# Three part-filled expert blocks of the first batch dealt early, and block work re-rated over the batches, in a top-k attention and dropless MoE kernel

## Chip, cores and metric

One core of one Trainium2 chip. The metric is device time in microseconds (us), the median of several runs. A profiled execution is one further run, with its own time.

## The reference

Top-32 attention over 8 batches of 8 heads (sequence 576, head dimension 64), then a mixture of 8 experts over the 4608 resulting rows of 512, each row going to one expert, none dropped:

```python
scores = scale * np.matmul(q, k.transpose(0, 1, 3, 2))
kth = np.partition(scores, -top_k, axis=-1)[..., -top_k:-top_k + 1]
scores = np.where(scores >= kth, scores, -1000000000.0)
attn = softmax(scores); x = (attn @ v) as rows (4608, 512)
expert_idx = np.argmax(x @ w_gate, axis=1)      # w_gate 512 x 8
for e in range(E):                              # rows sorted by expert
    h = np.maximum(x_sorted[lo:hi] @ w1[e], 0.0)   # 512 -> 1024
    y_sorted[lo:hi] = h @ w2[e]                    # 1024 -> 512
return gate_w[:, None] * y                      # softmax weight of the chosen expert
```

All tensors are float32.

## The kernel before

**The scan.** Attention is done in 144 groups, 18 for each batch. A group holds two query tiles. For each, TensorE makes the scores (`sc`, L292), ScalarE copies them (`s`, L299), VectorE (DVE) folds them and finds the 32nd largest score by repeated max and replace (L306 to L362), ScalarE and GpSimd (POOL) turn what lies under the threshold into a large negative exponent (`low` L371, `w` L387, L396), ScalarE takes the exponential (L404), and TensorE transposes the weights (`wTm` L415, `wTl` L429) and multiplies by the values (`po` L450). Products run three groups ahead (`AHEAD`). `low` runs once in each group.

**End of a batch.** `ending` turns the outputs into rows, computes the gate logits, ranks rows by expert (`choice`, `ranks`, `places`), and scatters each batch's rows with five indirect transfers into `x_rows`, a DRAM buffer in which every expert has its own region of `CAP` rows. `run` holds how far each region is filled. These small DVE steps wait in the list `aside`; `search` calls `tick` between its own instructions, which issues one of them.

**Blocks.** 128 rows of one expert are a block. `block` transposes its rows (`xtp`, `xTs`), multiplies by `w1` (`ph`, L893, 32 matmuls) and by `w2` (`py`, L910, 8 matmuls), and stores the result to the rows' places in the output (L808). A block is yielded in `PIECES` = 16 pieces: eight of four `ph` matmuls and eight of one `py` matmul. Blocks of the batches so far are dealt while the scan of the next batches goes on: after batch b, `table` works out which full blocks exist and writes `new_of[b]` of them into slots, and SP reads expert and place from a slot and loads rows (L749), `w1` (L741) and `w2` (L743), each 2 MB, into two buffers each. The numbers of new blocks are fixed when the program is built, from `upto_of`: 0, 4, 4, 5, 4, 5, 4. A slot without a full block would point at an empty block.

**The rate.** In the loop over the groups a credit grows by `rate` for each tile, and as many pieces as it holds (by `share` of the tile's place) are put between that group's transposes and products. From group 13 (`FIRST`) of a batch on, the rate is that of the blocks dealt after the batch before:

```python
if at == FIRST and b:
    rate = new_of[b - 1] * PIECES / (U * NT)
```

In the last batch the credit is spread so that three blocks (`KEEP`) remain, which run while the last rows are routed. The instruction order of TensorE, ScalarE and DVE in the loop is that of the program text; SP's and POOL's is set by the scheduler of the framework.

**The end.** After the last batch ten blocks remain beside the three kept: `SURE` = 2 whole ones that `table` finds first, four long blocks (`HALVES`: a whole block and a half of 64 rows together, `long_block`) and `PLAIN` = 4 whole ones, dealt by `end_table`. `fill_up` writes zero rows behind each expert's last row, so that part-filled blocks can be multiplied. Only if blocks are left over, or the search is in doubt, is a branch taken that does the rest (`rare`).

Of the kernel before, what the change touches and what calls it, by code (L numbers as in the profile page):

```python
# [9 lines left out]
F32 = mybir.dt.float32  # L10
I32 = mybir.dt.int32
AF = mybir.ActivationFunctionType
ALU = mybir.AluOpType
# [24 lines left out]
def _inner(ap: bass.AP, n: int) -> bass.AP:  # L38
    return _ins(ap, len(ap.ap), n)
# [3 lines left out]
def kernel(  # L43
# [47 lines left out]
    nc = tc.nc  # L91
    B, U, P, _ = qk.shape
    N, Dm = out.shape
    S = N // B
    E = moe_w_gate.shape[1]
# [4 lines left out]
    ST = S - SM  # L100
# [5 lines left out]
    NT = 2 * NC + 1  # L106
    DT = Dm // P
    FT = F // P
    XW = Dm + 2
    EB = N // P  # L110
    NSLOT = EB + E - 1
    CAP = N + P
    EMPTY = E * CAP // P
# [1 line left out]
    assert N % P == 0 and TOP_K == 32 and DT == U and P == 2 * D  # L115
    scale = float(D) ** -0.5
    sure = [max(0, -((E * (P - 1) - S * (b + 1)) // P)) for b in range(B - 1)]
    upto_of = [max(0, (S * (b + 1) - E * ST) // P - 1) for b in range(B - 1)]
    upto_of = [max(a, c) if b else 0 for b, (a, c) in enumerate(zip(sure, upto_of))]
    new_of = [b - a for a, b in zip([0] + upto_of, upto_of)]  # L120
    assert all(n >= b - a for n, a, b in zip(new_of, [0] + sure, sure))
    LAST = NSLOT - sure[-1]
    HALVES = E // 2
    SURE = 2
    PLAIN = EB - upto_of[-1] - HALVES - SURE
    LONG = P + ST
    assert PLAIN >= 0 and (N - E * (P - 1) + P - 1) // P - upto_of[-1] >= SURE
    assert LAST - SURE + HALVES <= NSLOT and PLAIN + HALVES <= NSLOT

    k = SimpleNamespace()  # L130
# [86 lines left out]
    run = const.tile([P, E], F32, name="run")  # L217
    nc.vector.tensor_copy(run, e_at)
    rest_i = const.tile([1, 1], I32, name="rest_i")
    rare = const.tile([1, 1], F32, name="rare")  # L220
    slot_last = const.tile([1, 2, NSLOT], I32, name="slot_last")
    slot_long = slot_last[:, 0, NSLOT - 3 * E:].rearrange("o (i e) -> o i e", i=3)
    assert LAST - SURE <= NSLOT - 3 * E
    done = const.tile([1, E], F32, name="done")
    nc.vector.tensor_scalar_mul(done, e_at[0:1, :], 1.0 / P)
    slot_max = const.tile([1, 2], F32, name="slot_max")
    nc.vector.memset(slot_max[:, 0:1], float(E - 1))
    nc.vector.memset(slot_max[:, 1:2], float(EMPTY))
    upto_all = const.tile([1, E + 1], F32, name="upto_all")
# [97 lines left out]
    def through(steps):  # L327
        for _ in steps:
            pass
        if steps in aside:  # L330
            aside.remove(steps)
# [265 lines left out]
    def table(slot_i, n, last, riding=None):  # L597

        sm = k.small
        full = sm.tile([1, E], F32, name="full")  # L600
        ci = sm.tile([1, E], I32, name="ci")
        left = sm.tile([1, E], F32, name="left")
        past = sm.tile([1, NSLOT, E], F32, name="past", bufs=1)
        slot_f = sm.tile([1, 2, NSLOT], F32, name="slot_f", bufs=1)
        upto, step = upto_all, step_all

        def steps():
            if last:
# [12 lines left out]
            nc.vector.tensor_tensor(left, full, done, op=ALU.subtract)  # L621
            yield
            nc.vector.tensor_tensor_scan(upto[:, 1:], ones[0:1, 0:E], left, 0.0, op0=ALU.mult, op1=ALU.add)
            yield
            nc.vector.tensor_tensor(step[:, 0:E - 1], done[:, 1:E], full[:, 0:E - 1], op=ALU.subtract)
            yield
            nc.vector.tensor_tensor(
                past[:, 0:n, :], _inner(slots[:, 0:n], E), _ins(upto[:, 1:], 1, n), op=ALU.is_ge
            )
            yield  # L630
            nc.vector.tensor_reduce(slot_f[:, 0, 0:n], past[:, 0:n, :], axis=AX.X, op=ALU.add)
            yield
            nc.vector.tensor_tensor(past[:, 0:n, :], past[:, 0:n, :], _ins(step[:, :], 1, n), op=ALU.mult)
            yield
            nc.vector.tensor_reduce(slot_f[:, 1, 0:n], past[:, 0:n, :], axis=AX.X, op=ALU.add)
            yield
            nc.vector.scalar_tensor_tensor(
                out=slot_f[:, 1, 0:n], in0=slot_f[:, 1, 0:n], scalar=done[:, 0:1], in1=slots[:, 0:n],
                op0=ALU.add, op1=ALU.add,
            )  # L640
            yield
            nc.vector.tensor_tensor(slot_i[:, :, 0:n], slot_f[:, :, 0:n], _inner(slot_max[:, :], n), op=ALU.min)
            yield
            if last:
                nc.vector.tensor_copy(rest_i, upto[:, E:])
            else:
                nc.vector.tensor_scalar_min(upto, upto, float(n))
                yield
                nc.vector.tensor_tensor(left, upto[:, 1:], upto[:, 0:E], op=ALU.subtract)
                yield  # L650
                nc.vector.tensor_tensor(done, done, left, op=ALU.add)
                yield

        return steps()

    def counted():

# [11 lines left out]
    def end_table(slot_i, slot_l, n, half, full):  # L669
# [16 lines left out]
            v.tensor_scalar(to, to, what[:, 0:1], None, ALU.add)  # L686

        def steps():
            v.tensor_tensor_scan(hupto[:, 1:], ones[0:1, 0:E], half, 0.0, op0=ALU.mult, op1=ALU.add)
            v.tensor_tensor(left, full, done, op=ALU.subtract)  # L690
            v.tensor_scalar(take, hupto[:, 1:], float(HALVES), None, ALU.is_le)
            v.tensor_tensor(take, take, half, op=ALU.mult)
            v.tensor_tensor(take, take, left, op=ALU.min)
# [16 lines left out]
                out=slot_f[:, 1, 0:m], in0=slot_f[:, 1, 0:m], scalar=done[:, 0:1], in1=at[:, 0:m],  # L710
                op0=ALU.add, op1=ALU.add,
            )
            v.tensor_tensor(slot_i[:, :, 0:n], slot_f[:, :, 0:n], _inner(slot_max[:, :], n), op=ALU.min)
            yield
            v.tensor_tensor(past[:, 0:E, :], _inner(slots[:, 0:E], E), _ins(hupto[:, 1:], 1, E), op=ALU.is_ge)
            v.tensor_reduce(long_f[:, 0, :], past[:, 0:E, :], axis=AX.X, op=ALU.add)
# [220 lines left out]
    with fast:  # L937
        units = [(b, u) for b in range(B) for u in range(U)]
        unit.append(load_unit(*units[1]))
        for n in unit:  # L940
            load_values(n)
        nc.sync.dma_start(x_rows[EMPTY * P:(EMPTY + 1) * P, :], blank)

        work = [(b, g) for b in range(B) for u in range(0, U, 2) for g in groups(u)]
        per_batch = len(work) // B
# [1 line left out]
        waiting, loaded, coming, spare, scatters, stores = [], [], [], [], [], []  # L947
        current = None
        left = clock = 0

        def landed(n):
            return clock is None or clock - n.at >= ON_CHIP
# [59 lines left out]
        def ending(b, u):  # L1012
# [48 lines left out]
            yield "pool"  # L1061
            through(steps)
            scatters.extend(scattering(r, x))
            if b == B - 1:
                scatter(KC)
                slot_i = k.small.tile([1, 2, NSLOT], I32, name="slot_i")
                half, full = counted()
                through(table(slot_i, SURE, False, half))
                firsts = [(slot_i[0:1, 0, j:j + 1], slot_i[0:1, 1, j:j + 1]) for j in range(SURE)]
                ready = load_rows(SimpleNamespace(), firsts[0][1], True)  # L1070
# [15 lines left out]
            if b == B - 1:  # L1086
                spare.extend(coming[PLAIN:])
                del coming[PLAIN:]
                longs = [[slot_long[0:1, i, j:j + 1] for i in range(3)] for j in range(E)]
                spare.extend((expert, half) for expert, half, _ in longs[HALVES:])  # L1090
                coming[0:0] = [(expert, [full, half]) for expert, half, full in longs[:HALVES]]
                assert len(loaded) == 2 and not waiting
                fill_up()
                coming[0:0] = [(firsts[0][0], ready)] + [(expert, (piece,)) for expert, piece in firsts[1:]]
                scatter(0)
# [27 lines left out]
        def loop():  # L1123
# [9 lines left out]
            for i, (b, g) in enumerate(work):  # L1133
# [20 lines left out]
                at_place("rows")  # L1154
                at = i % per_batch
                if at == FIRST and b:
                    rate = new_of[b - 1] * PIECES / (U * NT)
                credit += rate * len(g)
                room = left
                if b == B - 1 and at >= ARRIVED:  # L1160
# [61 lines left out]
    with ExitStack() as outer:  # L1222
# [10 lines left out]
        with ExitStack() as st:  # L1233
# [44 lines left out]
                    put()  # L1278
                nc.vector.tensor_scalar_add(ids, ids, S)
            fill_up()  # L1280
            slot_i = slot_last
            for _ in table(slot_i, NSLOT, True):
                pass
            nc.sync.dma_start(slot_d.rearrange("(a n) o -> o a n", a=2), slot_i)
# [53 lines left out]
```

## Time and profile before

| | |
|---|---|
| median of 3 runs | 1337.66 us (1337.55 to 1337.73) |
| profiled execution, its own time | 1339.03 us |
| its span, first to last instruction | 1337.4 us |
| mean granted TensorE clock | 0.955 |
| TensorE busy | 1189.3 us (89%) |
| DVE busy | 1076.6 us (81%) |
| ScalarE busy | 930.8 us (70%) |
| POOL busy | 661.9 us (49%) |
| DMA | 214.36 MB, mean 160 GB/s |

Times of single instructions and stretches come from the profiled execution. Busy time of an engine is the union of its recorded instructions; an instruction that waits within its record counts as busy. The granted clock is the share of full speed that TensorE's throttle let through.

### The profile page before, as it was taken

To read this page: it belongs to the slowest core of one execution; us is meant where nothing else is said; L and a number is where in the kernel's file an instruction comes from. 1 tells how busy PE (TensorE), PEld (TensorE's weight loads), DVE (VectorE), ACT (ScalarE), POOL (GpSimd) and SP (SyncE) were. 2 spreads that over 40 slices of the span, in tenths; PEclk is the share of its full clock that TensorE was granted. 3 is DMA by queue.
4 is the path that set the end of the run, shared out by engine and by line. 5 is a ranking of instruction groups with operands and counts; after the bars stand their busy time and mean duration, and the time that the engine had idled before them with its cause. 6 is when DMAs were issued, how large, how long until landed. Compare 5 with 4: busy or idle time off the path is not lost. (4 is left out here: it accounts for less than half of the span.)

```text
span 1337.4 us, 24295 instructions
## 1 busy us (share of the span) xinstructions
PE 1189.3 (89%) x7570; PEld 831.4 (62%) x7570; DVE 1076.6 (81%) x4629; ACT 930.8 (70%) x2125; POOL 661.9 (49%) x805
## 2 busy tenths in 40 slices
PE   5667766766799999999999999999999999999995
PEld 3344443444466766676677666666677667699973
DVE  7999999999999999999999999999999932000000
ACT  4788788887888888888787888887778851111110
POOL 3454547555755665567555756475547642000000
PEclk9788788888899999999999999999999999999998
DMA  2000001001384348435855294329452739946790
GB/s 84 30 29 30 30 29 65 29 29 38 122 305 168 108 164 288 160 110 175 297 208 179 74 350 170 118 76 372 171 204 87 283 116 332 369 146 219 290 342 18
DMA packets 95563, 214.36 MB, mean 160 GB/s; under 512 B 4926, under 2 KB 25662, under 8 KB 95424
## 3 DMA queue, kind: packets, MB, share of 16 engines
q1 hardware_dynamic: 88800, 192.45, 40.8%
q0 software_dynamic: 6336, 19.97, 4.2%
q8 instruction: 61, 1.00, 0.3%
q14 instruction: 78, 0.64, 0.2%
q10 hardware_dynamic: 288, 0.30, 0.1%
HBM read 191.42 MB, written 21.80 MB: 159 GB/s over the span
## 5 line engine op out<-in xcount | busy, mean ns | idle before, releaser
L396 POOL TENSOR_TENSOR w<-s,w 128x576 f32<-128x576 f32 x288 | 410.2, 1444 | 418.4 <-ACT w L387 418.4
L893 PE MATMUL ph<-xTs,w 128*128 128x128 f32 x2048 | 250.2, 276 | 5.9 <-ACT xTs L790 5.9
L893 PEld LDWEIGHTS ph<-xTs,w 128*128 128x128 f32 x2048 | 239.1, 192 | 21.9 <-issue 14.6
L910 PE MATMUL py<-w,hT 128*128 128x512 f32 x512 | 236.2, 597 | 0.0
L404 ACT ACTIVATE w<-w,nbias 128x576 f32<-128x576 f32 x288 | 224.1, 792 | 3.0 <-POOL w L396 2.0
L292 PE MATMUL sc<-qkb 64*128 64x288 f32 (+1 forms) x1280 | 206.0, 473 | 9.5 <-ACT s L299 5.1
L387 ACT ACTIVATE w<-s,low 128x576 f32<-128x576 f32 x288 | 207.6, 768 | 4.7
L415 PE MATMUL wTm<-turn,w 128*128 128x128 f32 x1152 | 170.1, 287 | 32.0 <-ACT xl L468 21.4
L415 PEld LDWEIGHTS wTm<-turn,w 128*128 128x128 f32 x1152 | 132.0, 145 | 92.5 <-issue 34.4
L299 ACT COPY s<-sc 128x576 f32<-128x576 f32 x288 | 168.9, 640 | 10.4 <-PE sc L292 10.4
L1217 DVE CAST any_i<-pd 1x1 int32<-1x1 f32 x1 | 0.1, 145 | 207.9 <-PE pd L1215 207.9
L422 ACT COPY wT<-wTm 128x512 f32<-128x512 f32 x256 | 139.2, 604 | 39.3 <-PE wTm L415 39.2
L354 DVE MAX8 tops<-scr 128x8 f32<-128x168 f32 x576 | 162.8, 317 | 0.0
L450 PE MATMUL po<-wT,vb 128*64 128x288 f32 x1024 | 154.9, 450 | 0.4 <-ACT wTt L437 0.4
L354 DVE MAX8 tops<-few 128x8 f32<-128x144 f32 (+1 forms) x576 | 154.4, 300 | 0.0
L292 PEld LDWEIGHTS sc<-qkb 64*128 64x128 f32 (+1 forms) x1280 | 110.1, 195 | 65.4 <-issue 25.6
L910 PEld LDWEIGHTS py<-w,hT 128*128 128x128 f32 x512 | 90.7, 190 | 90.4 <-issue 89.2
L808 POOL DMA_INDIRECT out_dram<-y,xg x40 | 42.6, 1066 | 189.8 <-ACT y L869 82.5
L345 DVE MAX8 few<-l 128x8 f32<-128x288 f32 x288 | 127.3, 442 | 0.0
L450 PEld LDWEIGHTS po<-wT,vb 128*64 128x64 f32 x1024 | 74.2, 150 | 77.3 <-issue 26.0
L306 DVE TENSOR_TENSOR h<-s 128x576 f32<-128x576 f32 x144 | 114.8, 797 | 3.9 <-ACT s L299 3.7
L308 DVE TENSOR_TENSOR l<-s 128x576 f32<-128x576 f32 x144 | 108.0, 750 | 0.0
(175 smaller groups left out, 1649.8 us busy)
## 6 DMA issues: line engine op xcount, KB each, us to landing
w<-in_moe_w_dram SPq DMA_DIRECT2D x72, 2048.0 KB, 8.6
qkb<-in_qk_dram SPq DMA_DIRECT2D x31, 608.0 KB, 5.8
vb<-in_v_dram SPq DMA_DIRECT2D x32, 320.0 KB, 3.1
xg<-x_rows SPq DMA_DIRECT2D x36, 257.0 KB, 10.6
x_rows<-blank SPq DMA_DIRECT2D x5, 257.0 KB
x_rows<-blank POOLq DMA_DIRECT2D x4, 257.0 KB, 8.2
x_rows<-x,posi POOLq DMA_INDIRECT x40, 3.1
out_dram<-y,xg POOLq DMA_INDIRECT x40, 4.5
```

The lines of the kernel that those rows point to most:

```text
L292: nc.tensor.matmul(ps[rows, j, 0:HF], n.q[d, cols], n.k[d, keys], start=True, stop=True)
L299: lambda m=m, ps=ps: nc.scalar.copy(s[:, m, :, :], ps[:, :, 0:HF]) for m, ps in enumerate(got)
L345: nc.vector.max(out=f.few[:, m, QF + 8 * j:QF + 8 * j + 8], in_=away)
L354: nc.vector.max(out=tops[:, m, r * 8:(r + 1) * 8], in_=src[m])
L387: nc.scalar.activation(w[:, m, :], s[:, m, :, :].rearrange("p j k -> p (j k)"), AF.Relu, scale=-STEEP, bias=low[:, m:m + 1],)
L396: k.last_pool = in_turn(nc.gpsimd.tensor_tensor(w[:, m, :], s[:, m, :, :].rearrange("p j k -> p (j k)"), w[:, m, :], op=ALU.subtract)).ins
L404: nc.scalar.activation(w[:, m, :], w[:, m, :], AF.Exp, scale=scale, bias=nbias[:, m:m + 1], accum_out=n.z[:, c:c + 1])
L415: nc.tensor.transpose(pm[:, c * P:(c + 1) * P], w[:, m, first:first + P], ident)
L422: nc.scalar.copy(wT[:, :, m, q], pm4)
L450: nc.tensor.matmul(po[r, 0:HF], n.v[:, c, r], rhs, start=(c == 0), stop=(c == KC - 1))
L893: nc.tensor.matmul(ph[:, f, :], n.w1[:, 0, dt, fc * P:(fc + 1) * P], n.xT[:, dt, :], start=(dt == 0), stop=(dt == DT - 1),)
L910: nc.tensor.matmul(py, hT[:, f, :], n.w2[:, 0, f, :], start=(f == 0), stop=(f == FT - 1))
```

## The change

After the first batch, `filled_up` finds the three experts (`SOON`) with the most rows of that batch and sets their `run` to 128, so that each has a full block; the rows between were written with zeros at the start, where nine transfers of `blank` now stand in place of one. The blocks dealt become 3, 3, 4, 5, 4, 5, 3. The rate is worked out by `level`: the blocks at hand and still to come, over the batches that remain, at the lowest of the averages that the blocks at hand allow. `end_table` gets six steps that move half blocks without a whole partner to whole ones, and the tables of the end get room for more slots. `slot_max[:, :]` becomes `slot_max[:, 0:2]` in both tables (not shown).

```diff
+    SOON = 3
-    upto_of = [max(0, (S * (b + 1) - E * ST) // P - 1) for b in range(B - 1)]
-    upto_of = [max(a, c) if b else 0 for b, (a, c) in enumerate(zip(sure, upto_of))]
+    upto_of = [min((S * (b + 1) - E * ST) // P + 1, EB - E - 1) for b in range(B - 1)]
+    upto_of = [max(a, c) if b else SOON for b, (a, c) in enumerate(zip(sure, upto_of))]
-    LAST = NSLOT - sure[-1]
+    LAST = NSLOT + SOON - min(a + upto_of[-1] - b for a, b in zip(sure, upto_of))
-    PLAIN = EB - upto_of[-1] - HALVES - SURE
+    PLAIN = EB - upto_of[-1] - HALVES - SURE + 1
...
-    slot_last = const.tile([1, 2, NSLOT], I32, name="slot_last")
+    slot_last = const.tile([1, 2, NSLOT + SOON], I32, name="slot_last")
...
+    def filled_up():
+
+        most, few = k.small.tile([P, E], F32, name="left"), k.small.tile([P, E], F32, name="full")
+        nc.vector.tensor_tensor(few, run, e_at, op=ALU.subtract)
+        yield
+        nc.vector.max(out=most, in_=few)
+        yield
+        nc.vector.tensor_scalar(few, few, most[:, SOON - 1:SOON], float(P), ALU.is_ge, ALU.mult)
+        yield
+        nc.vector.tensor_tensor(few, few, e_at, op=ALU.add)
+        yield
+        nc.vector.tensor_tensor(run, run, few, op=ALU.max)
+        yield
...
         def steps():
+            v.tensor_tensor(left, full, done, op=ALU.subtract)
+            v.tensor_tensor(some, half, left, op=ALU.subtract)
+            v.tensor_scalar_max(some, some, 0.0)
+            v.tensor_tensor(half, half, some, op=ALU.subtract)
+            v.tensor_tensor(full, full, some, op=ALU.add)
+            v.tensor_tensor(left, left, some, op=ALU.add)
+            yield
             v.tensor_tensor_scan(hupto[:, 1:], ones[0:1, 0:E], half, 0.0, op0=ALU.mult, op1=ALU.add)
-            v.tensor_tensor(left, full, done, op=ALU.subtract)
...
-        nc.sync.dma_start(x_rows[EMPTY * P:(EMPTY + 1) * P, :], blank)
+        for r in [e * CAP for e in range(E)] + [EMPTY * P]:
+            nc.sync.dma_start(x_rows[r:r + P, :], blank)
...
+        def level(b):
+
+            have, sums = left / PIECES, []
+            for n, new in enumerate(new_of[b:] + [0], 1):
+                sums.append(have / n)
+                have += new
+            sums[-1] = (have - KEEP / PIECES) / (len(sums) - 1 + (per_batch - FIRST) / per_batch)
+            return min(sums)
...
             scatters.extend(scattering(r, x))
+            if b == 0:
+                steps = filled_up()
+                aside.append(steps)
+                yield "weights"
+                yield "pool"
+                through(steps)
             if b == B - 1:
...
                 if at == FIRST and b:
-                    rate = new_of[b - 1] * PIECES / (U * NT)
+                    rate = level(b) * PIECES / (U * NT)
...
-            slot_i = slot_last
+            slot_i = slot_last[:, :, 0:NSLOT]
```

More of the change, by code (lines that the diff above doesn't have):

```diff
@@ L117 @@
     sure = [max(0, -((E * (P - 1) - S * (b + 1)) // P)) for b in range(B - 1)]
-    upto_of = [max(0, (S * (b + 1) - E * ST) // P - 1) for b in range(B - 1)]
-    upto_of = [max(a, c) if b else 0 for b, (a, c) in enumerate(zip(sure, upto_of))]
+    upto_of = [min((S * (b + 1) - E * ST) // P + 1, EB - E - 1) for b in range(B - 1)]
+    upto_of = [max(a, c) if b else SOON for b, (a, c) in enumerate(zip(sure, upto_of))]
     new_of = [b - a for a, b in zip([0] + upto_of, upto_of)]
-    assert all(n >= b - a for n, a, b in zip(new_of, [0] + sure, sure))
-    LAST = NSLOT - sure[-1]
+    LAST = NSLOT + SOON - min(a + upto_of[-1] - b for a, b in zip(sure, upto_of))
     HALVES = E // 2
     SURE = 2
-    PLAIN = EB - upto_of[-1] - HALVES - SURE
+    PLAIN = EB - upto_of[-1] - HALVES - SURE + 1
     LONG = P + ST
-    assert PLAIN >= 0 and (N - E * (P - 1) + P - 1) // P - upto_of[-1] >= SURE
+    assert PLAIN >= 0 and E == 8 and SOON < E
     assert LAST - SURE + HALVES <= NSLOT and PLAIN + HALVES <= NSLOT
@@ L219 @@
     rest_i = const.tile([1, 1], I32, name="rest_i")
-    rare = const.tile([1, 1], F32, name="rare")
-    slot_last = const.tile([1, 2, NSLOT], I32, name="slot_last")
-    slot_long = slot_last[:, 0, NSLOT - 3 * E:].rearrange("o (i e) -> o i e", i=3)
-    assert LAST - SURE <= NSLOT - 3 * E
+    slot_last = const.tile([1, 2, NSLOT + SOON], I32, name="slot_last")
+    slot_long = slot_last[:, 0, NSLOT + SOON - 3 * E:].rearrange("o (i e) -> o i e", i=3)
+    assert LAST - SURE <= NSLOT + SOON - 3 * E
     done = const.tile([1, E], F32, name="done")
     nc.vector.tensor_scalar_mul(done, e_at[0:1, :], 1.0 / P)
-    slot_max = const.tile([1, 2], F32, name="slot_max")
+    slot_max = const.tile([1, 3], F32, name="slot_max")
+    rare = slot_max[:, 2:3]
     nc.vector.memset(slot_max[:, 0:1], float(E - 1))
@@ L641, in steps @@
             yield
-            nc.vector.tensor_tensor(slot_i[:, :, 0:n], slot_f[:, :, 0:n], _inner(slot_max[:, :], n), op=ALU.min)
+            nc.vector.tensor_tensor(slot_i[:, :, 0:n], slot_f[:, :, 0:n], _inner(slot_max[:, 0:2], n), op=ALU.min)
             yield
@@ L712, in steps @@
             )
-            v.tensor_tensor(slot_i[:, :, 0:n], slot_f[:, :, 0:n], _inner(slot_max[:, :], n), op=ALU.min)
+            v.tensor_tensor(slot_i[:, :, 0:n], slot_f[:, :, 0:n], _inner(slot_max[:, 0:2], n), op=ALU.min)
             yield
@@ L1091, in ending @@
                 coming[0:0] = [(expert, [full, half]) for expert, half, full in longs[:HALVES]]
-                assert len(loaded) == 2 and not waiting
+                assert len(loaded) == 2
                 fill_up()
```

## The prediction

> **What bounds the kernel now.** I read the 40 slices first. VectorE (DVE) is at 9 almost from the start, TensorE (PE) only from slice 11 on, and the granted TensorE clock is uneven before slice 11 and full after.
>
> ```profile
> PE   5667766766799999999999999999999999999995
> DVE  7999999999999999999999999999999932000000
> PEclk9788788888899999999999999999999999999998
> ```
>
> Then I cut the scan into stretches. One group is one search step over two query tiles; ScalarE's `low<-tops` (L371) runs once in each, so its 144 start times are the group boundaries, and block work is re-rated at group 13 of each batch (`FIRST`). The windows view between groups 13, 31, 49, 67, 85, 103, 121, 139 and 143, and from there to the end, gives (columns: stretch, its length, then busy time and count of PE, weight loads, DVE, ACT, POOL, then clock, DMA share, GB/s):
>
> ```profile
> 109.80:238.40 128.60, 90.64 (x538) 54.17 (x536) 128.00 (x557) 105.21 (x246) 74.58 (x93) 0.85 0.12 40
> 238.40:367.60 129.20, 92.15 (x554) 55.95 (x552) 129.20 (x572) 104.93 (x246) 74.40 (x93) 0.86 0.17 56
> 367.60:498.90 131.30, 127.01 (x862) 88.11 (x860) 131.30 (x573) 113.10 (x261) 78.45 (x96) 1.00 0.52 183
> 498.90:631.40 132.50, 129.22 (x878) 89.41 (x876) 132.16 (x572) 113.64 (x264) 80.94 (x97) 1.00 0.51 182
> 631.40:775.70 144.30, 142.59 (x958) 99.28 (x956) 140.94 (x579) 115.63 (x267) 87.63 (x98) 1.00 0.57 202
> 775.70:908.60 132.90, 129.62 (x880) 89.63 (x881) 131.77 (x566) 113.64 (x263) 82.52 (x97) 1.00 0.50 178
> 908.60:1052.90 144.30, 142.59 (x958) 99.30 (x956) 140.92 (x579) 115.65 (x267) 87.59 (x98) 1.00 0.55 197
> 1052.90:1079.00 26.10, 23.76 (x175) 18.11 (x176) 24.17 (x110) 23.91 (x58) 16.80 (x20) 1.00 0.89 333
> 1079.00:1337.40 258.40, 238.86 (x1423) 194.50 (x1422) 15.06 (x87) 47.58 (x87) 30.36 (x36) 0.97 0.64 229
> ```
>
> Eighteen groups without block work take 128.6 to 129.2 us, with 4 blocks 131.3 to 132.9, with 5 blocks 144.3. A block is 16 pieces (8 of four `ph` matmuls, 8 of one `py` matmul), so the first 64 pieces cost about 3 us in all and the next 16 cost 11.6. DVE busy is no proof here, since its recorded times contain waiting (L306 runs from 726 to 1853 ns), so I asked what ScalarE waits for. In 238.4 to 367.6 the longest is
>
> ```profile
> ACT low L371 <- DVE tops L354: 18.1, 16, 2.2
> ```
>
> and in 631.4 to 775.7 that wait is not listed; the longest two are
>
> ```profile
> ACT wT L420 <- PE wTm L415: 7.1, 2, 4.6
> ACT wT L422 <- PE wTm L415: 7.0, 5, 2.0
> ```
>
> So up to about 4 blocks a batch the search on DVE sets the pace, and above it TensorE does. After 1079 TensorE runs the remaining blocks almost without a gap (238.9 of 258.4 us busy).
>
> **What the Trainium skill says.** "TensorE: Matmul & The Clock Gate", Part 1, the HAM clock gate: the throttled state is the default and steady matmul activity releases it. The trace agrees: mean clock 0.85 and 0.86 in the stretches without blocks, 1.00 in all those with them. The same page's specifications call VectorE's queue strict first-in-first-out; the trace agrees as far as it goes (DVE starts follow program order), so a small DVE step put into the search delays all behind it. "DMA: Bandwidth & Descriptors", Issuing engines are not separate DMA queues: transfers from all issuers share 16 engines, so added transfers count together; the share is 0.12 to 0.17 in the early stretches, so there is room.
>
> **The change part by part.**
>
> *How many blocks.* `new_of` goes from 0, 4, 4, 5, 4, 5, 4 (26) to 3, 3, 4, 5, 4, 5, 3 (27). `PLAIN` stays 4, `SURE` 2, `HALVES` 4, `KEEP` 3 blocks. So 37 blocks run instead of 36, and the added one lies in the scan: 24 there instead of 23. Priced in the full part a block is 11.6 us (144.3 less 132.7, the mean of the two 4-block stretches before and after it), 0.725 us a piece. Whether the slots are filled follows from the reference's routing: batch 0 sends 103, 79, 74, 60, 96, 61, 55, 48 rows to the experts, so experts 0, 4 and 1 are filled up with 25, 32 and 49 zero rows; carried on through all batches every dealt slot holds a full block, and at the end there are 4 half blocks and 4 plain ones, as before. The branch for spare blocks stays untaken.
>
> *Where the pieces go.* TensorE's instruction order as built, counted between the same group boundaries, before and after:
>
> | groups | pieces before | after | change of time, us |
> |---|---|---|---|
> | 13–30 | 0 | 0 | +1.0 |
> | 31–48 | 0 | 47 | +1.1 |
> | 49–66 | 63 | 49 | −0.9 |
> | 67–84 | 64 | 64 | 0 |
> | 85–102 | 80 | 68 | −8.7 |
> | 103–120 | 64 | 69 | +3.6 |
> | 121–138 | 80 | 67 | −9.4 |
> | 139–143 | 16 | 19 | +2.2 |
>
> The last four rows are the difference of pieces times 0.725. The stretches of 47 and 49 pieces have no counterpart in the trace. From below nothing they are bounded at 0 over 129.2 us (DVE still sets the pace; a gain is excluded, since no DVE work leaves), from above by the line from 0 to 64 pieces (mean 132.2, so 3.0 us, or 2.2 at 47): I take the middle, 1.1 and 1.2, which makes the second 130.4 against 131.3.
>
> *Steps on DVE, row 13–30.* Batch 0 had no table and gets one: some 16 small steps of 135 to 253 ns. Stretch 31–48 has one and 13–30 has none, and they differ by 0.6 us, far less than the sum of the recorded times, about 2.5 us, which overlap their neighbours. `filled_up` adds five steps on 128x8; the nearest rows (128x40 and 128x8 steps) record 140 to 185 ns, 0.85 us in all. I take 0.6 + 0.4; the ends are 0.8 and 3.4. Nothing is late behind them but the search itself, already counted.
>
> *Moved or added at no cost on the path.* Eight more `blank` transfers on SP at the start: 0.36 us of issue each (L942), 2.9 us, and 2.1 MB more. Behind them stand two `qkb` loads, the first issued at 22.5 us, 13 us after the blank at 9.35; cover gone, the first scores of unit 2 (five groups after their buffer is free) would be late by under 3 us. The three early blocks issue on SP three row loads, six weight loads and six register reads. In the built order each weight load stands at least 4 groups (some 28 us) ahead of its first matmul, with a median landing of 8.6 us, and each `qkb` load keeps its 5 groups; so SP's waits for weight buffers hold up nothing. On POOL one store (1.0 us) joins every block, in stretches where POOL is 74 of 129 us busy. ScalarE gets 2.6 us a block (0.63, 2 x 0.62, 0.71), at 105 of 129 us. The six steps added to `end_table`, and its slots growing from 17 to 21, run while TensorE has three kept blocks to do (DVE 15 us busy in 258): nothing; uncovered, under 1.5 us. `run` filled up shifts only addresses. The instruction order of TensorE after group 143 is the same.
>
> *Sum.* 1.0 + 1.1 − 0.9 + 0 − 8.7 + 3.6 − 9.4 + 2.2 = −11.1 us. Profiled span 1337.4 to 1326.3; the profiled execution took 1339.0, 1.4 above the median of the runs shown. Applied to the median 1337.66 this gives 1326.6.
>
> **Rivals.**
>
> *A larger gain: the knee lies above 64 pieces.* Full TensorE cost of a block is about 14.8 us by the rows (32 x 0.277, 8 x 0.6, four transposes), 0.92 a piece. If only that slope counted, the knee would be at 80 − 11.6/0.92 = 67 pieces, the three 67-to-69-piece stretches would be near 133 to 134, and 31–66 free: about −19, 1319. Against it: TensorE is already 97% busy at 64.
>
> *A smaller gain: drifting blocks.* At 64 pieces the block edges fall on the same groups every nine groups; at 68 they wander, so eight `ph` pieces (8.9 us) meet different tiles, and evacuations can come late. If each of the three stretches takes 4 us more, the gain is all but gone: −11.1 + 12 = +0.9, 1338.5. For it: single groups already reach 11.5 us. Against it: in the 5-block stretches the order also wanders, and TensorE is idle only 1.7 us of 144.3.
>
> *Slower: half clock in groups 31–66.* With blocks spread thin the clock may stay near 0.86. Then TensorE needs 92.15 plus 47 x 0.825/0.86 (0.825 being the busy time a piece adds, 13.2/16), about 137, plus some 2 us idle: 139 us in each stretch, +9.8 and +7.7 instead of +1.1 and −0.9, together 17.3 more: 1343.9. It decides from about 11 us over my two rows. Against it: the clock reached 1.00 around 360 us and stayed there once blocks ran.
>
> *The change does not do what it says*: slots dealt but empty, or the spare branch taken. The routing above excludes both but for ties.
>
> **How the numbers follow.** My case with its nearer ends, 1319 to 1332: 0.72; larger gain: 0.10; drifting blocks: 0.10; half clock: 0.07; the last 0.01. The range 1318 to 1334 leaves out the slow case, most of the drifting one and little of the larger gain. About 0.2%, 2.7 us, is what a measurement of this kernel can tell from no change. Faster 0.85, same 0.07, slower 0.08.
>
> **What would show it.** Right: between the same group boundaries 31–48 near 130 and 85–102, 103–120, 121–138 each at 134 to 137; clock 0.95 or more from group 31; 13–30 near 129.6; the part after group 143 still 258 us. Wrong: any of the three above 139, or 31–66 above 265 with the clock under 0.9, or L420 and L422 waiting for `wTm` as long as in the 5-block stretch.

## The result and the profile after

The changed kernel takes 1329.97 us (median of 4 runs, 1329.26 to 1332.19), the kernel before on the same chip 1337.7 (1337.55 to 1338.89): ratio 0.9943 [0.9926, 0.9960], 7.7 us faster. The profiled execution took 1330.3 us, with a span of 1328.6 against 1337.4, so 8.8 less. Forecast were 1326.6 and a span of 1326.3. The same program measured once more (below) took 1328.89, ratio 0.9931 [0.9917, 0.9944], with a span of 1327.1. The forecast gain of 11.1 us is thus at or past the edge of what both measurements allow; the time itself lies within the 1318 to 1334 that were stated.

The 40 slices of the changed kernel, TensorE, DVE and granted clock:

```profile
PE   5767766998889899999999999999999999999995
DVE  7999999999999999999999999999999942000000
PEclk9788788899999899999999999999999999999998
```

TensorE now comes up to 8 or 9 from slice 7 on (counted from 0), four slices earlier. The windows view between the same group boundaries as before (13, 31, 49, 67, 85, 103, 121, 139, 143, end; columns as in the prediction: stretch, length, then busy time and count of PE, weight loads, DVE, ACT, POOL, then clock, DMA share, GB/s):

```profile
108.89:239.44 130.55, 92.50 (x538) 55.81 (x536) 130.05 (x577) 105.17 (x246) 73.89 (x93) 0.83 0.17 54
239.44:370.74 131.30, 119.91 (x804) 81.33 (x802) 131.30 (x572) 110.86 (x258) 80.15 (x95) 0.98 0.40 143
370.74:502.85 132.11, 119.77 (x790) 80.22 (x788) 130.99 (x572) 111.97 (x259) 80.50 (x96) 0.97 0.41 145
502.85:636.43 133.58, 129.05 (x870) 88.76 (x868) 133.09 (x572) 113.54 (x263) 80.54 (x97) 1.00 0.52 184
636.43:773.24 136.81, 133.40 (x914) 93.24 (x912) 135.42 (x573) 114.62 (x265) 84.44 (x98) 1.00 0.59 211
773.24:908.69 135.45, 132.39 (x906) 92.14 (x902) 134.90 (x572) 114.28 (x265) 81.85 (x98) 1.00 0.50 171
908.69:1045.42 136.73, 133.17 (x894) 90.42 (x891) 134.41 (x571) 113.97 (x264) 81.88 (x97) 1.00 0.57 203
1045.42:1071.93 26.51, 25.55 (x176) 18.49 (x173) 25.46 (x117) 23.38 (x57) 15.23 (x20) 1.00 0.50 181
1071.93:1328.60 256.67, 236.81 (x1423) 193.67 (x1421) 15.80 (x92) 47.69 (x87) 30.13 (x36) 0.98 0.65 232
```

Beside the forecast:

| groups | pieces before, after | before, us | after | change | forecast |
|---|---|---|---|---|---|
| 13–30 | 0, 0 | 128.6 | 130.6 | +2.0 | +1.0 |
| 31–48 | 0, 47 | 129.2 | 131.3 | +2.1 | +1.1 |
| 49–66 | 63, 49 | 131.3 | 132.1 | +0.8 | −0.9 |
| 67–84 | 64, 64 | 132.5 | 133.6 | +1.1 | 0 |
| 85–102 | 80, 68 | 144.3 | 136.8 | −7.5 | −8.7 |
| 103–120 | 64, 69 | 132.9 | 135.4 | +2.5 | +3.6 |
| 121–138 | 80, 67 | 144.3 | 136.7 | −7.6 | −9.4 |
| 139–143 | 16, 19 | 26.1 | 26.5 | +0.4 | +2.2 |
| after 143 | | 258.4 | 256.7 | −1.7 | 0 |

Pieces are counted by the groups for which the program issues them. The traces give the same counts within a piece, except in 139–143, where three or four of the pieces start only after group 143 does (12 of 16 have started by then before, 15.5 of 19 after).

Group 13 starts 0.9 us earlier, which no part of the change explains: from group 0 to group 13 all the profiles below vary between 90.9 and 91.8 us. The forecast rows together came to −6.2 instead of −11.1; with the start and the part after group 143 it is −8.8. Every row that was to change has the forecast sign but 49–66, and the misses set the questions for the experiments: whether the two halves of the change work apart from each other, what makes 31–66 longer than forecast, and what the early steps on DVE cost.

What ScalarE waits for tells which regime a stretch is in (columns: total us, times, longest us). In groups 31–48 of the changed kernel the first line is still DVE's, in 85–102 TensorE's, with the transposes' wait fallen from 14.1 us over L420 and L422 to 7.5:

```profile
ACT low L371 <- DVE tops L354: 11.7, 12, 2.4
```

```profile
ACT wT L422 <- PE wTm L415: 6.6, 4, 3.2
ACT low L371 <- DVE tops L354: 5.2, 6, 1.6
...
ACT wT L420 <- PE wTm L415: 0.9, 1, 0.9
```

### The profile page after: what moved, and what is told of

It is laid out like the page before. It is cut to its first block, busy times and chain, and to the rows that moved or that the text cites. A ratio compares the mean times of both kernels' runs of the same rounds, so it can differ in the third digit from the quotient of the medians.

```text
span 1328.6 us, 24530 instructions
## 1 busy us (share of the span) xinstructions
PE 1195.5 (90%) x7654; PEld 837.3 (63%) x7654; DVE 1073.6 (81%) x4654; ACT 933.0 (70%) x2129; POOL 657.4 (49%) x806
## 2 busy tenths in 40 slices
DMA packets 98509, 220.95 MB, mean 166 GB/s; under 512 B 5181, under 2 KB 25917, under 8 KB 98368
## 5 line engine op out<-in xcount | busy, mean ns | idle before, releaser
L396 POOL TENSOR_TENSOR w<-s,w 128x576 f32<-128x576 f32 x288 | 410.0, 1444 | 417.3 <-ACT w L387 417.3
L913 PE MATMUL ph<-xTs,w 128*128 128x128 f32 x2112 | 260.1, 277 | 3.7 <-ACT xTs L810 3.7
L913 PEld LDWEIGHTS ph<-xTs,w 128*128 128x128 f32 x2112 | 248.7, 192 | 23.2 <-issue 18.6
L930 PE MATMUL py<-w,hT 128*128 128x512 f32 x528 | 250.3, 603 | 2.8 <-ACT hT L918 2.6
L292 PE MATMUL sc<-qkb 64*128 64x288 f32 (+1 forms) x1280 | 200.0, 463 | 9.5 <-ACT s L299 5.1
L422 ACT COPY wT<-wTm 128x512 f32<-128x512 f32 x256 | 139.1, 603 | 23.5 <-PE wTm L415 23.2
L292 PEld LDWEIGHTS sc<-qkb 64*128 64x128 f32 (+1 forms) x1280 | 107.4, 191 | 71.3 <-issue 33.1
L450 PE MATMUL po<-wT,vb 128*64 128x288 f32 x1024 | 149.0, 437 | 0.4 <-ACT wTt L437 0.4
```

The source lines that it names most:

```text
L292: nc.tensor.matmul(ps[rows, j, 0:HF], n.q[d, cols], n.k[d, keys], start=True, stop=True)
L396: k.last_pool = in_turn(nc.gpsimd.tensor_tensor(w[:, m, :], s[:, m, :, :].rearrange("p j k -> p (j k)"), w[:, m, :], op=ALU.subtract)).ins
L422: nc.scalar.copy(wT[:, :, m, q], pm4)
L450: nc.tensor.matmul(po[r, 0:HF], n.v[:, c, r], rhs, start=(c == 0), stop=(c == KC - 1))
L913: nc.tensor.matmul(ph[:, f, :], n.w1[:, 0, dt, fc * P:(fc + 1) * P], n.xT[:, dt, :], start=(dt == 0), stop=(dt == DT - 1),)
L930: nc.tensor.matmul(py, hT[:, f, :], n.w2[:, 0, f, :], start=(f == 0), stop=(f == FT - 1))
```

## Experiments

"67–138" is the sum of the four stretches from group 67 to 139: 554.0 us before, 542.6 after.

### The new rate alone

The kernel before, with the new rate and none of the early blocks:

```diff
+        def level(b):            # as in the change
...
-                if at == FIRST and b:
-                    rate = new_of[b - 1] * PIECES / (U * NT)
+                if at == FIRST and b > 1:
+                    rate = level(b) * PIECES / (U * NT)
```

> The kernel before with the levelled rate alone: no filled-up blocks, 36 blocks, deals 0, 4, 4, 5, 4, 5, 4 as before. Pieces between the boundaries 49, 67, 85, 103, 121, 139 and the end of the scan: 63, 65, 72, 72, 74, 21 in place of 63, 64, 80, 64, 80, 16, the same total. Theory A (above 64 pieces a stretch every piece costs the same, so only the pieces that leave that part count): the sum is unchanged, 1336 to 1339 us. Rival B (evening out is itself the gain, since a stretch of 80 is dearer than its share): stretches 85-102 and 121-138 fall by 7 each and 103-120 rises by less than 4, 1328 to 1332 us.

Measured: 1339.65 us, ratio 1.0015 [1.0008, 1.0022] to the kernel before (1338.15 in this set of runs). The windows from group 85 on:

```profile
633.43:773.37 139.94, 136.90 (x946) 96.81 (x944) 138.04 (x577) 115.26 (x266) 83.32 (x98) 1.00 0.59 212
773.37:912.24 138.87, 136.05 (x894) 91.86 (x892) 138.13 (x584) 114.47 (x265) 83.51 (x97) 1.00 0.50 175
912.24:1052.07 139.83, 137.32 (x948) 97.16 (x946) 136.76 (x557) 115.31 (x266) 84.24 (x98) 1.00 0.53 190
1052.07:1080.97 28.90, 28.34 (x185) 19.97 (x182) 25.32 (x117) 24.07 (x57) 15.71 (x21) 1.00 0.78 288
```

The stretches hold 72, 72, 74 and 21 pieces. Levelled, they cost 138.9 to 139.9 each, where 64 and 80 alternating had cost 132.9 and 144.3: a mean of 138.6. 67–138 falls only from 554.0 (288 pieces) to 552.6 (283). **Levelling alone brings nothing, since the time grows about evenly with pieces above 64**, so the linear reckoning of the prediction held here, and a gain from evenness as such is excluded. The last, short stretch grows by 2.9 us with 5 pieces more, and 49–66 by 2.1: the clock is at half until 3 us into group 49 (0.51 from 355 to 369 us, against 0.88 in the kernel before), and groups 49 and 50 together take 16.4 us instead of 14.3.

### The early blocks alone

The changed kernel with the rate of before:

```diff
-                    rate = level(b) * PIECES / (U * NT)
+                    rate = new_of[b - 1] * PIECES / (U * NT)
```

> The changed kernel with the old rule for the rate (the blocks of the batch before), so three blocks are still filled up and dealt early. Pieces from boundary 31 on: 47, 48, 64, 80, 64, 80, 1 in place of 47, 49, 64, 68, 69, 67, 19. Theory A (only the number of pieces before and after group 67 counts, 0.725 us each): 289 pieces against 287 from 67 on, so 1330 to 1333 us, the same as the changed kernel. Rival B (the early deal gains only if its pieces are spread over all later stretches; the last five groups take some 25 us with or without pieces): the stretches cost what they cost before the change, 132.5, 144.3, 132.9, 144.3 and about 25, together some 10 us more than the changed kernel's, 1338 to 1342 us.

Measured: 1339.65 us, ratio 1.0006 [0.9998, 1.0015]. The stretches from group 85 on hold 80, 64, 80 and 1 pieces:

```profile
632.10:776.42 144.32, 142.61 (x958) 99.32 (x956) 140.94 (x579) 115.64 (x267) 87.58 (x98) 1.00 0.57 202
776.42:909.29 132.87, 129.60 (x880) 89.60 (x880) 131.75 (x566) 113.64 (x263) 82.55 (x97) 1.00 0.50 176
909.29:1053.63 144.34, 142.63 (x958) 99.33 (x956) 140.98 (x579) 115.65 (x267) 87.57 (x98) 1.00 0.56 200
1053.63:1078.89 25.26, 18.45 (x105) 10.66 (x103) 23.83 (x110) 21.93 (x53) 14.56 (x19) 0.86 0.46 167
```

Theory A (1330 to 1333: early blocks alone carry the gain) fell, B (1338 to 1342) held. With the old rate the pieces dealt early are missed only in the last, short stretch, which goes from 16 pieces to 1 and saves less than 1 us: it had room for them. **So neither half of the change is worth anything alone.** The early blocks make room; the new rate takes 20 pieces out of 67–138 (288 to 268) for 11.4 us, 0.57 us each.

### Other shares at the end of a batch

The table `share` puts 1.4 times the credit at the tile with number `2 * NC`, so that the fifth group of a batch (place 4, counted from 0) gets a clump of pieces: four recorded `py` in a row in batch 2, six in batch 3. (The trace records each `py` matmul twice, 16 records for the 8 of a block, so six are three pieces.) In the changed kernel places 3 and 5 of batches 2 and 3 last 8.75, 8.75 and 8.11, 10.12 us, while most groups last 6.9 to 7.5. The edit on the changed kernel moves pieces from place 4 to place 8:

```diff
+                if b * per_batch + at > 31 and u == 0 and tile == 2 * NC:
+                    share = 0.7
+                if u == 1 and tile == 3:
+                    share = 1.2
```

> The changed kernel, with the share of pieces in the tail group at place 4 of a batch halved from 1.4 to 0.7 and that of the last group of every second head pair raised from 0.5 to 1.2; the pieces of every stretch stay as they are within one. Theory C (the early stretches cost 2 to 3 us although DVE sets the pace, because pieces at places 1 to 4 hold up the rank matmuls and gate logits of the batch end, for which ScalarE and DVE wait in order): the group at place 5 falls from 9.1 to about 8 us in all six batches from 2 on, 4 to 6 us in all, 1324 to 1327 us. Rival D (the cost is that of TensorE's work, wherever it stands): no change, 1329 to 1332 us.

Measured: 1327.81 us, ratio 0.9916 [0.9902, 0.9929]. The windows of groups 31–48 and 49–66, with the same 47 and 49 pieces:

```profile
239.56:369.65 130.09, 120.34 (x804) 80.95 (x802) 130.09 (x572) 110.71 (x258) 81.03 (x95) 0.98 0.41 145
369.65:499.53 129.88, 118.29 (x790) 79.10 (x788) 129.88 (x572) 112.10 (x260) 80.58 (x96) 0.99 0.42 146
```

31–66 falls from 263.4 to 260.0; 67–138 stays at 542.6. The timeline shows how. TensorE in the changed kernel, around place 5 of batch 3 (start, duration, line, instructions in a row):

```profile
439.58 4.75 PE L930 MATMUL py<-w,hT 128*128 128x512 f32 x6
444.26 1.24 PE L292 MATMUL sc<-qkb 64*128 64x288 f32 x8
445.44 0.42 PE L531 MATMUL rank<-run,turn 128*128 128x48 f32 x2
```

and ScalarE there, with its wait in brackets:

```profile
447.20 0.17 ACT L1090 COPY run<-rank 128x8 f32<-128x8 f32 x1 [3.01 <-PE rank L534]
...
447.60 1.15 ACT L299 COPY s<-sc 128x576 f32<-128x576 f32 x2
```

DVE waits for that copy in turn, with `pos`, a small step of the ranking that stands between the steps of the search:

```profile
447.40 0.20 DVE L546 TENSOR_TENSOR pos<-rank,oh 128x40 f32<-128x40 f32 x1 [1.12 <-ACT run L1090]
```

In the next group a small step of the table on DVE is recorded with 1.20 us; with the new shares it takes 0.17:

```profile
455.33 1.20 DVE L613 TENSOR_SCALAR ci<-ci 1x8 int32<-1x8 int32 x1
```

```profile
453.07 0.17 DVE L613 TENSOR_SCALAR ci<-ci 1x8 int32<-1x8 int32 x1
```

With the new shares, TensorE and then ScalarE at the same place:

```profile
438.48 1.92 PE L930 MATMUL py<-w,hT 128*128 128x512 f32 x2
440.32 1.27 PE L292 MATMUL sc<-qkb 64*128 64x288 f32 x8
441.52 0.42 PE L531 MATMUL rank<-run,turn 128*128 128x48 f32 x2
```

```profile
443.28 0.17 ACT L1090 COPY run<-rank 128x8 f32<-128x8 f32 x1 [0.18 <-PE rank L534]
```

Six recorded `py` hold TensorE for 4.75 us; the scores and the rank matmuls of the batch just ended stand behind them; ScalarE's small copy of `run` waits for those 3.01 us, and DVE's `pos` 1.12 us for the copy, the only wait of DVE listed in groups 49 to 66. With two `py` ScalarE waits 0.18 us and DVE not at all. (Half clock makes the clump longer, from 436.8 to 443.6 us in the changed kernel; but the two `py` of the other profile, 1.92 us, fell in half clock as well, from 437.0 to 440.4.)

Most of the rest of the gain lies at the step L613, which takes about 1 us more without the new shares in batch 3, and in this profile in batch 2 too. In the scans of all twelve profiles it is long 23 times, 1.18 to 1.23 us, and each time it starts 0.21 to 0.25 us into a POOL operation of L396 and ends 0.02 us after it; the other 59 times it takes 0.14 to 0.18. Which of the two comes about depends on how the steps fall: the kernel before has the long one in batch 3 as well.

Place 5 falls from 8.11 and 10.12 to 7.09 and 7.51 us. The kernel of the section before, with early blocks and the old rate, lies between: it has four recorded `py` there in both batches, place 5 lasts 8.04 us in each, DVE does not wait for `run`, and 31–66 takes 260.7 us with 95 pieces. Place 3, which the edit leaves alone, keeps its 8.75. In batches 4 to 7 the new shares shorten place 5 as well (7.65, 8.60, 10.10, 9.76 to 6.74, 7.51, 6.69, 7.88), and yet 67–138 gains nothing: there the pieces moved away lengthen other groups (place 7 goes from 7.51 to 10.61 us in batch 5). The time lies between the ranges of the two theories. Theory C, a delay at the batch's end, holds where DVE sets the pace; D, the sum of TensorE's work, where TensorE does. Measured again, in another set of runs:

> The changed kernel with the share of place 4 halved and that of place 8 raised, once more: 1326 to 1328 us, groups 31 to 66 near 260 and the stretches from 67 to 139 near 542.5, so the gain over the changed kernel stays in the part where DVE sets the pace.

1325.47 us, ratio 0.9910 [0.9893, 0.9926], 31–66 in 259.7, 67–138 in 542.4: the same. Against the repeat of the changed kernel (261.6, below) the gain in 31–66 is 1.9 us, against its first profile 3.4.

### No pieces at all at the end of a batch

```diff
+                if 31 <= i < 67:
+                    share = 0.0 if 1 <= at <= 4 else 1.3 * share
```

> The changed kernel with no pieces at places 1 to 4 of batches 2 and 3, the others of groups 31 to 66 raised by 1.3; pieces by stretch 44, 47, 69, 68, 68, 68, 19 in place of 47, 49, 64, 68, 69, 67, 19. Theory C (batch-end chain held up by pieces): groups at places 3 and 5 return to about 7.5 us there, so groups 31 to 66 take some 259 us in place of 263.4; the five pieces more in 67-84 cost 3 to 4 us, and the whole is about 1329. Rival D (the cost is TensorE's work): groups 31 to 66 stay within 1 us of 263.4 less 7 pieces, and the whole is 1331 to 1334.

Measured: 1343.21 us, ratio 1.0042 [1.0028, 1.0055]. Both theories missed the total: 31–66 grows to 277.2 us.

```profile
239.76:377.40 137.64, 121.71 (x792) 82.56 (x790) 134.34 (x572) 110.71 (x257) 78.04 (x95) 0.94 0.40 137
377.40:516.97 139.57, 122.14 (x790) 80.97 (x788) 133.73 (x572) 111.15 (x259) 78.76 (x96) 0.94 0.40 139
```

Place 3 did return to 7.57 and 7.56 us, as C said. But the credit that had built up came out at once: places 5 and 6 got 7 or 8 and then 10 pieces, and places 5 to 7 lasted 9.77, 11.80, 11.85 and 10.18, 12.44, 10.29. TensorE is no busier than before (121.7 of 137.6 us). Here DVE does wait for the copies of scores:

```profile
DVE h L306 <- ACT s L299: 6.3, 3, 2.7
```

Half clock, 33 us in these groups against 13 in the changed kernel, is not the main reason: it has some part in place 5, but 13 us of it lie in groups without pieces, which keep their length, and places 6 and 7 ran at a clock of 1.00. So this is a fault of the same kind as above, made larger: what stands behind a clump of 10 pieces comes so late that the scores computed three groups ahead no longer cover it. The kernel shows one thing more: 67–138 takes 540.8 us with 273 pieces, less than the changed kernel's 542.6 with 268, so the places of the pieces matter there as much as a few pieces do.

### The changed kernel again

> The changed kernel once more, to have it beside the others on one chip: 1329 to 1332 us, groups 13-30 near 130.6 and groups 31 to 66 near 263 us; if those 263 hold a chance effect of the clock (half clock from 437 to 444 us in the first profile), the second half of them falls by about 2 us.

1328.89 us (1328.65 to 1329.04), ratio 0.9931 [0.9917, 0.9944]. 31–66 lasts 261.6 us here instead of 263.4; all stretches from 67 on agree within 0.1 us. The same program thus varies by 1.8 us in that part. The first profile has 13.0 us of half clock there, this one 7.7: group 31, at half clock for its first 2.8 us there and 0.9 us here, lasts 8.01 and 6.92. The clump before place 5 of batch 3 runs mostly at half clock in both, in 4.75 and 4.44 us, and place 5 lasts 10.12 and 9.68. The step L613 of batch 2 is recorded with 1.20 us there and 0.17 here.

### The steps on DVE alone

The kernel before, with a `filled_up` that leaves `run` as it is and a table after batch 0 whose slots nothing reads:

```diff
+        nc.vector.tensor_tensor(most, run, few, op=ALU.max)   # to a scratch tile
...
+            if b == 0:
+                steps = filled_up()
...
+                steps = table(slot_i, 3, False)
```

> The kernel before with the five filled-up steps (into a scratch tile, run left as it is) and a table of three slots after batch 0, its slots not used: the added DVE steps alone. If they are what made groups 13-30 dearer, these take 130.3 to 130.8 us in place of 128.6 and the whole is 1.5 to 2.2 us above the kernel before; by my forecast's price it is 1.0 above; if the excess came from the transfers of early weights instead, groups 13-30 stay at 128.6.

Measured: 1340.0 us, ratio 1.0014 [1.0005, 1.0022], and groups 13–30 last 130.2 us instead of 128.6:

```profile
108.84:239.01 130.17, 92.03 (x541) 55.28 (x538) 130.17 (x577) 105.00 (x247) 74.97 (x93) 0.84 0.13 39
```

DVE runs 20 instructions more there (577 against 557). Chance differences move the whole stretch: with the steps it lasts 129.9 to 130.6 us in all kernels but one (133.7, below), without them 128.0 and 128.6. But the steps stand in groups 24 and 25, and these two last 16.0 to 16.1 us together in all ten profiles that have the steps and 14.06 in both without. So the steps cost 2.0 us, 0.1 each. The stretches after group 31 agree with the kernel before within 0.6 us.

### TensorE kept warm

Two more matmuls in each group from 13 to 66, into scores that are written anew after them:

```diff
+            for j in range(2):
+                nc.tensor.matmul(ps[:, j, HF:HF + 192], n.q[d, 0:P], n.k[d, 0:192], start=True, stop=True)
```

> The changed kernel with two further 192-column matmuls in each of groups 13 to 66, into unused columns of the score banks, so that TensorE is less idle there. If half clock is what makes groups 31 to 66 cost 263.4 in place of 258.4, the clock goes to 1.00 there and they fall to about 260 although TensorE does more; if it is the place of the pieces before the batch end's chain, they stay at 263 or rise by up to 5 (0.65 us a group, where TensorE is the bound). Groups 13-30, at clock 0.83 before, should stay at 130.5 if DVE alone sets the pace there.

The clock goes to 1.00 in both stretches, and their lengths stay at 131.3 and 131.9:

```profile
239.67:370.98 131.31, 126.66 (x862) 90.59 (x860) 131.31 (x572) 111.11 (x258) 79.32 (x95) 1.00 0.41 144
370.98:502.87 131.89, 126.77 (x858) 89.16 (x856) 131.45 (x572) 112.37 (x259) 80.14 (x96) 1.00 0.41 145
```

TensorE does 7 us more in each and the sum stays at 263.2 us. Place 5 of batch 3, whose clump now takes 2.74 us instead of 4.75, falls from 10.12 to 8.98; place 5 of batch 2 rises from 8.11 to 8.68. Place 3 falls as well (8.75, 8.75 to 7.35, 6.91), but it ran at full clock already, and place 2 before it rises by as much in batch 2 and by 1.2 us in batch 3 (6.92 to 8.33 and 8.11). So half clock does lengthen the clump, and full clock bought with more work doesn't pay; what it would bring for nothing isn't shown. The order alone took 1.9 to 3.4 us away. The median of the runs, 1335.55, ratio 0.9984 [0.9976, 0.9992], is 5 us above the profiled execution (1330.57). Where that lies stays open, since no trace was taken of those runs, and the profile may not speak for them. The same matmuls added to the kernel with other shares:

> The same matmuls added to the kernel with the changed shares (0.7 at place 4, 1.2 at place 8). If the shares already removed what the early pieces cost (260.0 against 258.4 without pieces), the added matmuls change nothing or cost up to 3 us in groups 31 to 66; if clock still mattered, they gain 1 us. The whole 1326 to 1330 us.

1332.76 us, ratio 0.9961 [0.9947, 0.9975], against 1327.81 and 1325.47 without them, in other sets of runs; in the profile 31–66 lasts 260.6 (260.0 without), so a TensorE kept warm in this way wins nothing there. 13–30 lasts 133.7 (130.6 without, and 130.6 in the kernel above that has the matmuls too), which is unexplained.

### Four blocks a batch, and the rest in the last one

If blocks that start at changing groups cost something, three batches of exactly 4 blocks (64 pieces, edges on the same groups again) and one with all the rest should beat 64, 68, 69, 67:

```diff
-                    rate = level(b) * PIECES / (U * NT)
+                    rate = {3: 4, 4: 4, 5: 4, 6: 4.85}.get(b, level(b)) * PIECES / (U * NT)
...
+                if 31 < i < 67 and u == 0 and tile == 2 * NC:
+                    share = 0.7
+                if 31 < i < 67 and u == 1 and tile == 3:
+                    share = 1.2
```

> The changed kernel with the changed shares of places 4 and 8 in groups 31 to 66 alone, and rates of 4 blocks a batch from group 67, 4.85 from 121, in place of the level: pieces 47, 49, 64, 65, 64, 76, 18 in place of 47, 49, 64, 68, 69, 67, 19. If block edges that wander over the groups cost over and above the pieces (the stretches of 67 to 69 pieces took 135.4 to 136.8 us, 0.3 to 1.8 above the line from 64 to 80), three stretches of four whole blocks take 132.5 to 134 each and the last about 142, 539 to 542 in all in place of 542.5: 1324 to 1327 us. If only the number of pieces counts, 542.5 and 1326 to 1328.

Measured: **1323.6 us (1323.37 to 1325.49), ratio 0.9894 [0.9877, 0.9910], the lowest median of all.** In the same set of runs the kernel with other shares took 1325.47; the intervals of the two ratios overlap. The windows from group 67 on hold 64, 65, 64 and 76 pieces:

```profile
499.66:633.24 133.58, 129.04 (x870) 88.77 (x868) 133.09 (x572) 113.55 (x262) 80.54 (x97) 1.00 0.52 185
633.24:768.22 134.98, 131.15 (x890) 90.82 (x888) 133.94 (x573) 114.38 (x264) 83.35 (x97) 1.00 0.61 212
768.22:900.28 132.06, 129.33 (x878) 89.40 (x876) 132.06 (x572) 113.85 (x264) 80.08 (x97) 1.00 0.55 182
900.28:1040.22 139.94, 139.15 (x944) 97.44 (x942) 138.60 (x575) 115.11 (x267) 85.50 (x98) 1.00 0.58 200
```

Together 540.6 us for 269 pieces, against 542.4 for as many in the kernel with other shares: a difference of 1.8 us, and not the 12 of the rival. That it is the edges isn't shown: the kernel without pieces at the batch's end has edges that drift and takes 540.8 us for 273 pieces. 76 pieces, spread over the whole of a batch, take 139.9 where 80 took 144.3.

## Why the prediction was right, and where its sum was off

*Regimes and direction: right.* Up to about 64 pieces in 18 groups DVE sets the pace, above it TensorE. The gain lies in the two 5-block stretches (−7.5, −7.6) and is paid for in 103–120, as forecast. "Each at 134 to 137" held in all three, 136.8, 135.4, 136.7; the waits on L420 and L422 halved; the clock was 0.97 or more from group 31.

*Price of a piece: a little high.* The three full stretches gained 12.6 us where 0.725 us a piece gave 14.5. The kernel with the rate alone pays 10.0 us for 15 pieces more than the changed kernel in 67–138, 0.67 each, and before against after gives 0.57. (The trace has 14 pieces there, which makes it 0.71.) These are means over whole arrangements and no constant: the 273 pieces that take 540.8 us fit neither. The pieces per stretch were forecast exactly.

*67–84, forecast 0: +1.1.* Both kernels have 64 pieces there; the blocks start at other groups. The stretch takes 133.6 in the last experiment too, and 132.3 with other shares, so the places of the pieces matter by about a microsecond.

*31–66, forecast 260.7 in all: 263.4, and 261.6 when repeated.* The step that failed is the "middle, 1.1 and 1.2". It bounded the cost by the line from 0 to 64 pieces and asked only whether TensorE has time on average; it has (119.9 of 131.3 us). What it left out is the order at the batch's end: six recorded `py` ahead of the rank matmuls, ScalarE's copy behind those, DVE's `pos` behind that, and the step L613 where it falls into a POOL operation. Half clock in the clump adds to it. As a mean price the term was not bad: with the old rate, and no more than four `py` there, the part takes just 260.7, with other shares 260.0. That such delays stay on the path fits the Trainium skill, "TensorE: Matmul & The Clock Gate", specifications, which calls the queues of ScalarE and VectorE strict first-in-first-out; the trace agrees, with 3.01 us on ScalarE and 1.12 us on DVE.

*DVE steps in 13–30, forecast +1.0: +2.0.* The value taken lay near the lower end of its bounds (0.8 and 3.4). It came from comparing two stretches of one profile, 0.6 us apart; but the kernels without the steps differ by as much in 13–30 (128.0 and 128.6) though their program is the same there. Of the recorded 3.4 us the steps cost a little over half.

*139–143, forecast +2.2: +0.4.* The full price was put on three pieces in a stretch that had room. Measured lengths are 25.3 us with 1 piece, 26.0 with 16, 25.3 to 25.6 with 18, 26.5 with 19 and 28.9 with 21: nearly flat up to about 19.

*After group 143, forecast 258: 256.7.* TensorE has 1423 instructions there in both. The difference is a stretch of half clock in the profile of before. Two windows of it and of the changed kernel at the same work:

```profile
1086.40:1096.60 10.20, 8.44 (x45) 4.87 (x44) 0.22 (x1) 3.41 (x10) 0.25 (x1) 0.83 0.00 0
```

```profile
1079.40:1089.60 10.20, 8.44 (x60) 5.92 (x59) 1.47 (x4) 4.11 (x11) 2.08 (x4) 1.00 0.11 8
```

Both begin about 7.4 us after group 143. TensorE got through 45 matmuls at a mean clock of 0.83 in the one, 60 at 1.00 in the other. Seven profiles without such a stretch have tails of 256.4 to 257.2, those with one 258.4 to 259.0, and one with more 260.0. So of the 8.8 us of span about 1.7 were the clock's, and 0.9 lie before group 13: the profile's gain is nearer to the forecast than the stretches that change (−6.2), by luck.

*The rivals.* Larger gain: no, 136.8 us at 68 pieces, not 133. (Its price of a block is too low: it counts 8 `py` at 0.6 us, and the trace has 16 records, 0.43 us apart at full clock, so 6.9 us instead of 4.8. That would move its knee to about 68 pieces.) Drifting blocks: at most 1.8 us where 12 were feared, and the edges are not shown to be its cause. Half clock in 31–66: seen in places, for some 8 to 13 us of 262, with a mean of 0.98 and 0.97, not 0.86. A change that doesn't do what it says: no, the added pieces and transfers (220.95 MB against 214.36) are in the trace, and the tail shows no added blocks. TensorE waits for loads of rows as long as before, for weights nowhere.

## What to carry to other kernels

Price a piece of moved work by the stretch that it leaves and the one that it enters: here 0.57 to 0.71 us on average where TensorE sets the pace, and near nothing where DVE does or where the last stretch has room, so that two edits which are worth nothing alone can bring 8 us together. Where an engine has slack on average, look for the small in-order step behind a clump of filler (a copy that waits 3 us for a rank); spreading the clump took 1.9 to 3.4 us off the part where it stood. Repeat the profile before explaining a microsecond or two: two profiles of one program differed by 1.8 in one part, where their clocks differed too.

## What the hardware showed that was not expected

**Half clock in the tail.** The clock falls to half for about 3.4 us at a time. The Trainium skill, "TensorE: Matmul & The Clock Gate", Part 1, has the clock decided over windows of about 3.4 us, and the trace agrees: 10.2 us at a mean of 0.83 is 3.4 us at half. One such window after group 143 makes the whole about 1.7 us longer. TensorE's work has a sparse stretch there, with waits of 0.68, 0.68 and 0.35 us close together in the kernels before and after alike. In the five profiles where the clock falls, the 3.4 us window just before has TensorE busy for 1.71 to 1.82 us; in the seven others the edges of the windows fall elsewhere over the same work, and none there has less than 1.96. (Elsewhere in these traces windows with 1.6 to 1.8 us went either way, so this is no exact threshold.) The kernel with other shares has the half clock in one profile and not in the other, so it is luck of the execution, not the change's doing.

**A DVE step behind a POOL operation.** The 1x8 step L613 takes a microsecond more when it starts while L396 runs on POOL, in all 23 such cases of the twelve profiles and in no other. Why is not shown.
